# Seven products in the first and the last block of a split FFN: ten more pairs of one kernel

## The chip, the cores and the metric

The kernel runs on one core of one Trainium2 chip. The metric is the device time of one execution in microseconds (us). TensorE is called PE here (its weight loads PEld), VectorE DVE, ScalarE ACT, GpSimd POOL, and the queue that issues the transfers SP.

## The reference

Attention with 8 batches of 576 tokens and 8 heads (half of them with a local mask, half with a strided one) gives a matrix x of 4608 tokens by 512. Behind it stands a feed-forward layer:

```
h = x @ w_in            # 512 -> 2048
g = h * np.cos(h)
return (g @ w_out).astype(np.float32)     # 2048 -> 512
```

All of it is in float32. The change concerns the last line alone.

## The kernel before

The kernel has a long first phase (attention and x @ w_in, which leaves h in DRAM) and a second phase, g @ w_out. The second phase is what the change touches.

**Blocks and pairs.** The 4608 tokens are cut into 18 blocks of 256 (`NTB`), block s being 0 to 17. The 2048 hidden features are cut into 8 pairs of 128-feature tiles (`NF`), pair f being 0 to 7. One step of the second phase, "pair (s, f)", multiplies the 256 tokens by 256 features of g with the 256 by 512 weights of that pair and adds the result to the block's banks in PSUM. The steps stand in the order of `tiles`: all pairs of block 0, then of block 1, and so on.

**Precision.** Every operand is split in a high part (`g_hi`, rounded by ACT) and a low part (`g_lo`, the rest, subtracted by POOL or by DVE), line 188. A product is hi x hi + hi x lo + lo x hi. In `pair` all matmuls with `g_hi` stand first, then `halfway()`, then those with `g_lo`. So `g_lo` is wanted only some way into the pair.

**Eight products or seven.** A pair is a 2 by 2 block product. The plain way takes eight block products; they are issued as 12 matmuls of 512 columns. The other way (Strassen-Winograd) takes seven, issued as 21 matmuls of 256 columns, and needs sums of g and sums of the weights. The weights' sums are made once in the first phase, kept in DRAM (`t_all`) and split by `split_sums`. The sums of g are made for each pair in `gate` by POOL: three additions (lines 681, 682, 685), and then one split of 896 columns in place of one of 512. `seven(s, f)` says which pairs take seven products: those of `SEVEN` (4, 5, 6, 1, 2), not in block 0, not in block 17, and in block 1 only 4, 5 and 6. Pairs 0, 3 and 7 always take eight, and DVE rather than POOL makes their `g_lo` (`BY_VECTOR`).

**What sets the order.** `ahead(at)` starts the stages of `gate` for later pairs while pair `at` is emitted; `LEADS` says how many pairs earlier each stage is started. In the first steps of the second phase, POOL has more to do than gates: `made` places there the splits of the last six weight tiles (`output_weights`, three of them on POOL, at steps 0, 2 and 4) and the splits of the weights' sums for pairs 1 and 2 (`split_sums`, 768 columns and then 256, twice). Program order is the emission order, rearranged by the framework's scheduler before the run; each engine then executes its own list strictly in order. `by_gpsimd` keeps the gates' POOL instructions in the order of the pairs.

**Banks.** A block with any pair of seven has four banks (`lower`, `upper`, `more`, `most`) of the five seats; `shared` adds `more` and `most` up after pair 6, and `store` adds them to `lower` and `upper` on DVE. A block without such a pair has two banks, and `store` copies them out.

Of the kernel before, what the change touches and what calls it, by code (L numbers as in the profile page):

```python
# [19 lines left out]
ALU = mybir.AluOpType  # L20
# [61 lines left out]
NTB = NTOK // TB  # L82
SEVEN = (4, 5, 6, 1, 2)
ROWS = (0, 3, 7)


LEADS = ((6, 4, 3, 2), (7, 4.5, 3.5, 2))
AHEAD = tuple(PER_BATCH - n for n in (20, 17, 13, 10, 7, 3))

BY_VECTOR = (0, 3, 7)  # L90
# [6 lines left out]
SUMMED = (14, 28, 36)  # L97
LATE = 6
# [8 lines left out]
def attention_cos_ffn(ctx, tc, qkl, vl, qkvs, w_in, w_out, eye, eye16, mask_l0, mask_l, mask_s, out):  # L107
    nc = tc.nc
# [484 lines left out]
    def output_weights(room, n, rest=nc.gpsimd):  # L593
        both = room()
        t = weight_tile(n // 2).rearrange("p l m n -> p l (m n)")
        nc.sync.dma_start(out=both, in_=w_all[n])
        yield
        split(both, t[:, 0], t[:, 1], rest=rest)
        wo.append((t[:, 0], t[:, 1]))
        yield  # L600
# [20 lines left out]
    def split_sums(room, n):  # L621

        t = room()
        nc.sync.dma_start(out=t, in_=t_all[n])
        yield
        t = t.rearrange("p (j n) -> p j n", j=4)
        most = wp.tile([P, 2, 3, 2 * P], F32R, name="v")
        split(t[:, :3], most[:, 0], most[:, 1])
        sums[SEVEN[n]] = [(most[:, 0, n], most[:, 1, n]) for n in range(3)]
        yield  # L630
        if n % 3 == 0:
            lasts.append(wp.tile([P, 2, 3, 2 * P], F32R, name="v"))
        last = lasts[-1][:, 0, n % 3], lasts[-1][:, 1, n % 3]
        split(t[:, 3], *last)
        sums[SEVEN[n]].append(last)
        yield
# [1 line left out]
    wo, lasts, gates, sums = [], [], {}, {}  # L638

    def seven(s, f):  # L640
        return 0 < s < NTB - 1 and f in SEVEN[:len(SUMMED) if s == 1 else len(SEVEN)]

    of_gates = []

# [5 lines left out]
    def gate(s, f):  # L650
# [18 lines left out]
        if not seven(s, f):  # L669
            low, pool = (wave, nc.vector) if f in BY_VECTOR else (r, nc.gpsimd)  # L670
            nc.vector.tensor_tensor(out=low, in0=wave, in1=h, op=ALU.mult)
            yield
            g_hi, g_lo = (gp.tile([P, 7 * P], F32R, name=name) for name in ("g_hi", "g_lo"))
            lo = split(low, g_hi[:, :4 * P], g_lo[:, :4 * P], rest=pool)
            if pool is nc.gpsimd:
                by_gpsimd(lo)
            gates[s, f] = g_hi, g_lo
            yield
# [15 lines left out]

    def ahead(at):
        for i, tile in enumerate(tiles):
            if i - at in LEADS[seven(*tile)]:
                next(work[i])

    class Outputs:  # L700
# [17 lines left out]
        def pair(self, f, g_hi, g_lo, halfway):  # L718

            w1, w2 = wo[2 * f:2 * f + 2]  # L720
            if seven(self.s, f):
                left, right = slice(0, 2 * P), slice(2 * P, 4 * P)
                plain = {name: [w[:, part] for w in both] for name, both, part in (
                    ("b11", w1, left), ("b21", w2, left), ("b22", w2, right),
                )}
                products = [
                    (n, plain[w] if w in plain else sums[f][w], (name, at, at + 1)) for n, w, name, at in OUTPUTS
                ]
            else:
                products = [  # L730
                    (2 * n + half, w, (name, 0, 2)) for half, name in enumerate(("lower", "upper"))
                    for n, w in enumerate((w1, w2))
                ]
            groups = [products]
            if self.last and f == NF - 1:
                groups = [products[:2], *(
                    [(n, [w[:, 2 * P * i:2 * P * (i + 1)] for w in both], ("upper", i, i + 1))
                     for n, both, _ in products[2:]] for i in range(2)
                )]
            for group in groups:  # L740
                for n, both, to in group:
                    for w in both:
                        self.add(*to, g_hi[:, n * P:(n + 1) * P], w)
                if group is groups[0]:
                    halfway()
                for n, (w, _), to in group:
                    self.add(*to, g_lo[:, n * P:(n + 1) * P], w)
# [14 lines left out]
        def store(self):  # L762

            rows = out[self.s * TB:(self.s + 1) * TB, :].rearrange("(h p) d -> h p d", h=2)
            for half, name in enumerate(("lower", "upper")):
                o = op.tile([P, 2, 2 * P], F32, name="o", bufs=4)
                if "more" in self.banks:
                    nc.vector.tensor_tensor(
                        out=o, in0=self.banks[name], in1=self.t[:, 2 - 2 * half:4 - 2 * half], op=ALU.add
                    )  # L770
                parts = (slice(0, 1), slice(1, 2)) if self.last and half else (slice(0, 2),)
                for i, part in enumerate(parts):
                    if "more" not in self.banks:
                        copy = nc.scalar.copy if half == i else nc.vector.tensor_copy
                        copy(out=o[:, part], in_=self.banks[name][:, part])
                    nc.sync.dma_start(
                        out=rows[half].rearrange("p (n d) -> p n d", n=2)[:, part], in_=o[:, part]
                    )
# [10 lines left out]
    with ExitStack() as phase:  # L789
# [18 lines left out]
        m, n, o = ((pools[name], name) for name in "mno")  # L808
# [67 lines left out]
        for n in range(2, NF):  # L876
            for i in range(2):
                at = 7 * n + 7 * i // 2 - 13
# [5 lines left out]
        for n in range(NFC - LATE):  # L884
            at = (B - 1) * PER_BATCH + STEP * (n // 2) + 12 + 3 * (n % 2)
# [6 lines left out]
        for b in range(1, B):  # L892
            for i, (summed, made) in enumerate(PREPARED):
                at = (b - 1) * PER_BATCH
# [5 lines left out]
        for slot in range(max(*plan, *steps) + 1):  # L900
            b, at = divmod(slot, PER_BATCH)
            if slot in plan:
                plan[slot]()
            for units_at in bursts.get(slot, ()):
                burst(*units_at)
            for unit in turns.get(slot, ()):
                next(unit)
            for step in steps.get(slot, ()):
                step()
            if b == B - 1:  # L910
                if at == 0:
                    attention.close()
                    sg = ctx.enter_context(tc.tile_pool(
                        name="sg", bufs=3, space=bass.MemoryType.PSUM, side="right", reuse_waits="tile"
                    ))
                    gap(ctx, "to_gates", 56, side="right")
                    gp, hp, rp = (
                        ctx.enter_context(tc.tile_pool(name=name, bufs=bufs, side="right", reuse_waits="tile"))
                        for name, bufs in (("gp", 3), ("hp", 5), ("rp", 3))
                    )  # L920
                if at in AHEAD:
                    ahead(AHEAD.index(at) - len(AHEAD))
# [3 lines left out]
    op = ctx.enter_context(tc.tile_pool(name="op", bufs=2, reuse_waits="tile"))  # L926
# [6 lines left out]
    made = {}  # L933
    for n in range(NFC - LATE, NFC):
        rest = nc.vector if n % 2 else nc.gpsimd
        weights = output_weights(lambda: tp.tile([P, DM], F32, name="both", bufs=LATE), n, rest)
        next(weights)
        made[n + LATE - NFC] = [weights]
    for n in range(len(SUMMED), len(SEVEN)):
        weights = split_sums(lambda: tp.tile([P, 2 * DM], F32, name="t", bufs=2), n)  # L940
        next(weights)
        for i in range(2):
            made.setdefault(LATE + 2 * (n - len(SUMMED)) + i, []).append(weights)
    for i, (s, f) in enumerate(tiles):
        if f == 0:
            block = Outputs(s)
        ahead(i)
        for step in made.get(i, ()):
            next(step, None)
        block.pair(f, *gates.pop((s, f)), partial(ahead, i + 0.5))  # L950
        if "more" in block.banks and f >= max(SEVEN):
            if f == max(SEVEN):
                shared = block.shared()
            next(shared, None)
        if f == NF - 1:
            block.store()
# [94 lines left out]
```

## Time and profile before

| | us |
|---|---|
| timed runs (three) | 852.77, 851.85, 852.76; median 852.76 |
| the profiled execution, its own time | 851.99 |
| its span, first to last instruction | 850.2 |
| outside the span | 1.8 |
| busy: PE / PEld / DVE / ACT / POOL | 839.9 / 783.9 / 554.9 / 529.8 / 536.3 |
| second phase on PE, first to last matmul | 473.42 to 846.64 |

Starts are counted in us from the start of the span. A row of a timeline is one instruction, or several equal ones in a row, with its start and its duration. Instructions on one engine overlap slightly, so what one instruction costs its engine in a full queue is the distance from its start to the start of the next, not its duration.

### The profile page before, as it was taken

Reading aid. Unit: us, or ns where it says so; the run is one execution under the profiler, and the core shown is the slowest. Engines: PE = TensorE matmul, PEld = TensorE weight load, DVE = VectorE, ACT = ScalarE, POOL = GpSimd, SP = SyncE. Lnnn points to the kernel's source line nnn. Section 1 sums busy time; section 2 is a strip of 40 time slices with the busy share of each in tenths; the row PEclk is TensorE's granted clock in tenths of the full one; section 3 lists DMA queues with packets and bytes.
Section 4 is the critical chain, followed back from the end, with each engine's and each line's share of the span. In section 5 each row is a group of like instructions: output and inputs, shape, how many; then the busy total and the mean of one; then the engine's idle time right before and its main releaser. Section 6 shows DMA issues by size and latency. Waiting matters only on the chain.

```text
span 850.2 us, 23162 instructions
## 1 busy us (share of the span) xinstructions
PE 839.9 (99%) x9147; PEld 783.9 (92%) x9147; DVE 554.9 (65%) x1090; ACT 529.8 (62%) x1031; POOL 536.3 (63%) x543
## 2 busy tenths in 40 slices
PE   8899999999999999999999999999999999999998
PEld 5799999999999999999999889999999999999996
DVE  5777655667667576677333667777777776767671
ACT  3766545555445454454457877777777777777772
POOL 3569984415215243163265588999998989898951
PEclk9999999999999999999999999999999999999999
DMA  9788444566674765846465844444444444444330
GB/s 325 230 268 295 148 164 151 190 231 213 209 260 163 246 224 189 301 159 218 176 220 199 281 125 136 124 127 135 125 127 134 125 126 131 130 124 144 116 125 26
DMA packets 91901, 151.82 MB, mean 179 GB/s; under 512 B 8464, under 2 KB 53008, under 8 KB 91792
## 3 DMA queue, kind: packets, MB, share of 16 engines
q1 hardware_dynamic: 91072, 150.11, 53.9%
q8 instruction: 72, 1.18, 0.6%
q10 hardware_dynamic: 720, 0.23, 0.1%
q14 instruction: 37, 0.30, 0.1%
HBM read 96.30 MB, written 54.00 MB: 177 GB/s over the span
## 4 chain that ended last, share of the span: by engine, by line
PE 96%; DMA 1%; POOL 1%; ACT 1%; DVE 1%; issue 1%; SPq 0%
PE q L716 44%; PE m L539 21%; PE n L539 10%; PE m L510 6%; PE o L539 5%; PE acc L342 2%; PE acc L407 2%; PE acc L325 2%; PE acc L394 1%; DMA v<-in_qkvs 1%; PE acc L377 1%; PE m L325 0%; POOL x_lo L188 0%; PE o L394 0%; ACT w L187 0%
## 5 line engine op out<-in xcount | busy, mean ns | idle before, releaser
L716 PE MATMUL q<-w,g_hi 128*128 128x512 f32 (+1 forms) x1000 | 199.9, 338 | 0.0
L716 PEld LDWEIGHTS q<-w,g_hi 128*128 128x128 f32 x1000 | 159.7, 188 | 22.1
L188 POOL TENSOR_TENSOR g_lo<-g,g_hi 128x896 fp32r<-128x896 f32 x78 | 165.1, 2131 | 6.3 <-ACT g_hi L187 6.0
L716 PE MATMUL q<-w,g_lo 128*128 128x512 f32 (+1 forms) x500 | 111.4, 338 | 0.0
L539 PE MATMUL m<-x_hi,v 128*128 128x288 f32 x448 | 109.3, 299 | 0.5 <-ACT m L547 0.5
L539 PE MATMUL m<-x_hi,w 128*128 128x288 f32 x448 | 108.4, 298 | 0.0
L662 DVE SCALAR_TENSOR_TENSOR r<-wave,h_in 128x512 f32<-128x512 int32 x144 | 96.0, 684 | 15.3 <-ACT wave L661 13.9
L664 ACT ACTIVATE wave<-r,quarter 128x512 f32<-128x512 f32 x144 | 98.5, 688 | 6.0 <-DVE r L662 5.9
L187 ACT CAST g_hi<-g 128x896 fp32r<-128x896 f32 x78 | 73.4, 941 | 39.6 <-POOL g L685 27.6
L716 PEld LDWEIGHTS q<-w,g_lo 128*128 128x128 f32 x500 | 82.7, 188 | 10.9
L661 ACT ACTIVATE wave<-h_in 128x512 int32<-128x512 f32 x144 | 83.6, 591 | 7.6 <-DVE g_lo L188 7.4
L716 PE MATMUL q<-v,g_hi 128*128 128x256 f32 x624 | 85.4, 279 | 0.0
L295 POOL TENSOR_TENSOR pn_s<-e_sb,mx 128x324 f32<-128x324 f32 x28 | 21.0, 749 | 100.1 <-DVE mx L293 85.3
L539 PEld LDWEIGHTS m<-x_hi,v 128*128 128x128 f32 x448 | 78.1, 188 | 1.6 <-ACT m L547 0.7
L539 PEld LDWEIGHTS m<-x_hi,w 128*128 128x128 f32 x448 | 78.0, 188 | 0.8
L716 PEld LDWEIGHTS q<-v,g_hi 128*128 128x128 f32 x624 | 78.3, 188 | 0.0
L547 ACT COPY m<-m 128x288 f32<-128x288 f32 x112 | 44.5, 398 | 48.9 <-PE m L539 42.9
L188 DVE TENSOR_TENSOR g_lo<-wave,g_hi 128x512 fp32r<-128x512 f32 x54 | 37.2, 689 | 53.3 <-PE q L716 33.5
L539 PE MATMUL m<-x_lo,v 128*128 128x288 f32 x224 | 66.1, 295 | 0.0
L539 PE MATMUL m<-x_lo,w 128*128 128x288 f32 x224 | 65.9, 294 | 0.0
L682 POOL TENSOR_TENSOR g<-g 128x256 f32<-128x256 f32 x78 | 57.7, 740 | 6.1
L680 DVE TENSOR_TENSOR g<-wave,h_in 128x512 f32<-128x512 f32 x78 | 52.8, 683 | 12.7 <-ACT wave L664 12.7
(138 smaller groups left out, 1996.9 us busy)
## 6 DMA issues: line engine op xcount, KB each, us to landing
h_all<-h SPq DMA_DIRECT2D x128, 288.0 KB, 2.9
h_in<-h_all SPq DMA_DIRECT2D x144, 256.0 KB, 2.8
qk<-in_qkvs SPq DMA_DIRECT2D x28, 324.0 KB, 4.4
out<-o SPq DMA_DIRECT2D x35, 256.0 KB, 3.1
qk<-in_qkl SPq DMA_DIRECT2D x21, 416.0 KB, 4.6
raw<-in_w_in SPq DMA_DIRECT2D x16, 512.0 KB, 4.4
raw<-in_w_out SPq DMA_DIRECT2D x16, 512.0 KB, 5.3
v<-in_vl SPq DMA_DIRECT2D x24, 224.0 KB, 4.3
```

Source lines behind the costliest of these rows:

```text
L187: with_product(cast(out=hi, in_=x))
L188: return rest.tensor_tensor(out=lo, in0=x, in1=hi.bitcast(F32), op=ALU.subtract)
L295: nc.gpsimd.tensor_tensor(out=pn, in0=e, in1=z[:, :n].unsqueeze(2).broadcast_to([P, n, w]), op=ALU.mult)
L510: in_turn(nc.tensor.matmul(self.banks[i, j], a[:, c * P:(c + 1) * P], y[:, c], start=k == 0 and m == 0, stop=k == 1 and m == len(ops) - 1, ...
L539: in_turn(nc.tensor.matmul(bank, a[:, c * P:(c + 1) * P], y[:, c], start=first and i == 0, stop=i == len(ops) - 1, skip_group_check=True,))
L547: nc.scalar.copy(out=t, in_=self.bank[name[0]])
L661: with_product(nc.scalar.activation(out=k, in_=h, func=AF.Copy, scale=1.0 / (2.0 * math.pi), bias=0.25))
L662: nc.vector.scalar_tensor_tensor(out=r, in0=k, scalar=-2.0 * math.pi, in1=h, op0=ALU.mult, op1=ALU.add)
L664: sin = nc.scalar.activation(out=wave, in_=r, func=AF.Sin, bias=quarter)
L680: nc.vector.tensor_tensor(out=g[:, :4].rearrange("p n t -> p (n t)"), in0=wave, in1=h, op=ALU.mult)
L682: by_gpsimd(pool.tensor_tensor(out=g[:, 5:7], in0=g[:, 0:5:4], in1=g[:, 1:2].broadcast_to([P, 2, P]), op=ALU.subtract))
L716: in_turn(nc.tensor.matmul(at, a, w, start=first, stop=True, skip_group_check=True))
```

## The change

Three things are changed. `seven` now takes seven products for pairs 4, 5 and 6 of block 0 as well, and for all five pairs of `SEVEN` in every later block, so for pairs 1 and 2 of block 1 and for all five in the last block: ten pairs more. The stages of the gates of those three pairs of block 0 get a row of leads of their own. The splits of the weights' sums for pairs 1 and 2 stand two steps sooner (steps 4 to 7 rather than 6 to 9), as block 1 now uses them. `store` adds part by part, since the last block stores its upper half in two parts.

```
-LEADS = ((6, 4, 3, 2), (7, 4.5, 3.5, 2))
+LEADS = ((6, 4, 3, 2), (7, 4.5, 3.5, 2), (7, 4, 3.5, 2))
...
     def seven(s, f):
-        return 0 < s < NTB - 1 and f in SEVEN[:len(SUMMED) if s == 1 else len(SEVEN)]
+        return f in SEVEN[:len(SEVEN) if s else len(SUMMED)]
+
+    def leads(s, f):
+        return LEADS[2 if seven(s, f) and not s else seven(s, f)]
...
         for i, tile in enumerate(tiles):
-            if i - at in LEADS[seven(*tile)]:
+            if i - at in leads(*tile):
                 next(work[i])
...
                 o = op.tile([P, 2, 2 * P], F32, name="o", bufs=4)
-                if "more" in self.banks:
-                    nc.vector.tensor_tensor(
-                        out=o, in0=self.banks[name], in1=self.t[:, 2 - 2 * half:4 - 2 * half], op=ALU.add
-                    )
                 parts = (slice(0, 1), slice(1, 2)) if self.last and half else (slice(0, 2),)
                 for i, part in enumerate(parts):
-                    if "more" not in self.banks:
+                    if "more" in self.banks:
+                        nc.vector.tensor_tensor(
+                            out=o[:, part], in0=self.banks[name][:, part],
+                            in1=self.t[:, 2 - 2 * half:4 - 2 * half][:, part], op=ALU.add,
+                        )
+                    else:
...
-            made.setdefault(LATE + 2 * (n - len(SUMMED)) + i, []).append(weights)
+            made.setdefault(LATE - 2 + 2 * (n - len(SUMMED)) + i, []).append(weights)
```

The lists of three engines show where this puts instructions. First POOL before, from the first weight split of the second phase (the one that the trace shows at 477.14 us) on. `w` are weight tiles, `v` the weights' sums, `g_lo` of 512 columns the splits of pairs 4, 5, 6 of block 0 and of pairs 1 and 2 of block 1.

```order
L188 TENSOR_TENSOR w_7936<-both_7935,w_7936 128x512
L188 TENSOR_TENSOR w_7942<-both_7941,w_7942 128x512
L188 TENSOR_TENSOR g_lo_8012<-r_7963,g_hi_8011 128x512
L188 TENSOR_TENSOR w_7948<-both_7947,w_7948 128x512
L188 TENSOR_TENSOR g_lo_8038<-r_7991,g_hi_8037 128x512
L188 TENSOR_TENSOR g_lo_8064<-r_8017,g_hi_8063 128x512
L188 TENSOR_TENSOR v_8129<-t_7953,v_8129 128x768
L188 TENSOR_TENSOR v_8156<-t_7953,v_8156 128x256
L188 TENSOR_TENSOR v_8187<-t_7955,v_8187 128x768
L188 TENSOR_TENSOR g_lo_8145<-r_8095,g_hi_8144 128x512
L188 TENSOR_TENSOR v_8156<-t_7955,v_8156 128x256
L188 TENSOR_TENSOR g_lo_8182<-r_8123,g_hi_8181 128x512
```

Now POOL in the changed kernel, from the same weight split on. `g_7982`, `g_8012` and `g_8044` are the gates of pairs 4, 5 and 6 of block 0 (their three additions are lines 684, 685 and 688 now), `g_lo_8022` is the split of pair 4.

```order
L188 TENSOR_TENSOR w_7938<-both_7937,w_7938 128x512
L684 TENSOR_TENSOR g_7982<-g_7982 128x128
L685 TENSOR_TENSOR g_7982<-g_7982 128x256
L688 TENSOR_TENSOR g_7982<-g_7982 128x128
L684 TENSOR_TENSOR g_8012<-g_8012 128x128
L188 TENSOR_TENSOR w_7944<-both_7943,w_7944 128x512
L685 TENSOR_TENSOR g_8012<-g_8012 128x256
L688 TENSOR_TENSOR g_8012<-g_8012 128x128
L188 TENSOR_TENSOR g_lo_8022<-g_7982,g_hi_8021 128x896
L684 TENSOR_TENSOR g_8044<-g_8044 128x128
L188 TENSOR_TENSOR w_7950<-both_7949,w_7950 128x512
L188 TENSOR_TENSOR v_8089<-t_7955,v_8089 128x768
```

It goes on with the rest of pair 6's additions, the splits of pairs 5 (`g_lo_8054`) and 6 (`g_lo_8078`), and the additions of pair 1 of block 1 (`g_8149`) around the second set of weights' sums.

```order
L685 TENSOR_TENSOR g_8044<-g_8044 128x256
L188 TENSOR_TENSOR v_8131<-t_7955,v_8131 128x256
L688 TENSOR_TENSOR g_8044<-g_8044 128x128
L188 TENSOR_TENSOR g_lo_8054<-g_8012,g_hi_8053 128x896
L188 TENSOR_TENSOR g_lo_8078<-g_8044,g_hi_8077 128x896
L684 TENSOR_TENSOR g_8149<-g_8149 128x128
L188 TENSOR_TENSOR v_8171<-t_7957,v_8171 128x768
L685 TENSOR_TENSOR g_8149<-g_8149 128x256
L188 TENSOR_TENSOR v_8131<-t_7957,v_8131 128x256
L688 TENSOR_TENSOR g_8149<-g_8149 128x128
```

So the first set of weights' sums now stands ahead of the split of pair 5 of block 0, where it stood behind the split of pair 6. Behind these rows come the additions of pair 2 of block 1, the splits of its pairs 1 and 2, the additions of pairs 4 and 5, the split of pair 4, the additions of pair 6, and the splits of pairs 5 and 6.

At the end of DVE's list there stood one copy of the last part, behind the last gate's work:

```order
L671 TENSOR_TENSOR r_12562<-wave_12563,h_in_12516 128x512
L662 SCALAR_TENSOR_TENSOR r_12584<-wave_12585,h_in_12542 128x512
L671 TENSOR_TENSOR wave_12585<-wave_12585,h_in_12542 128x512
L188 TENSOR_TENSOR g_lo_12619<-wave_12585,g_hi_12618 128x512
L775 COPY o_12667<-q3_12523 128x256
```

and now stand the sums of the last block and three additions (the last row is two instructions):

```order
L757 TENSOR_TENSOR t_12785<-q0_12628,t_12785 128x256
L759 TENSOR_TENSOR t_12785<-q4_12639,t_12785 128x512
L762 TENSOR_TENSOR t_12785<-q4_12639,t_12785 128x256
L773 TENSOR_TENSOR o_12808<-q1_12598,t_12785 128x512
L773 TENSOR_TENSOR o_12811<-q3_12603,t_12785 128x256 x2
```

ACT's two copies at the end (one of 512 columns, one of 256) are gone.

## Rows read from the trace of the kernel before

**Rows 1.** The page: span, busy time of the engines, granted PE clock by slices.

```profile
span 850.2 us, 23162 instructions
PE 839.9 (99%) x9147; PEld 783.9 (92%) x9147; DVE 554.9 (65%) x1090; ACT 529.8 (62%) x1031; POOL 536.3 (63%) x543
PEclk9999999999999999999999999999999999999999
```

**Rows 2.** The page: the chain that ended last, share of the span by engine.

```profile
PE 96%; DMA 1%; POOL 1%; ACT 1%; DVE 1%; issue 1%; SPq 0%
```

**Rows 3.** Waits of PE, whole span, longest and shortest: total, times, longest.

```profile
PE acc L342 <- issue: 2.0, 1, 2.0
...
PE m L325 <- issue: 0.2, 1, 0.2
```

**Rows 4.** Timeline of PE: starts of pairs (0, 4) and (0, 7).

```profile
484.52 2.03 PE L716 MATMUL q<-w,g_hi 128*128 128x512 f32 x8
...
492.93 2.01 PE L716 MATMUL q<-w,g_hi 128*128 128x512 f32 x8
```

**Rows 5.** Timeline of PE: block 1, pairs 1, 3, 4, 5 and 7.

```profile
498.40 2.03 PE L716 MATMUL q<-w,g_hi 128*128 128x512 f32 x8
...
504.01 2.01 PE L716 MATMUL q<-w,g_hi 128*128 128x512 f32 x8
...
506.76 0.86 PE L716 MATMUL q<-w,g_hi 128*128 128x256 f32 x6
...
508.40 0.51 PE L716 MATMUL q<-w,g_lo 128*128 128x256 f32 x3
...
509.22 0.86 PE L716 MATMUL q<-w,g_hi 128*128 128x256 f32 x6
...
514.12 2.01 PE L716 MATMUL q<-w,g_hi 128*128 128x512 f32 x8
```

**Rows 6.** Timeline of POOL, start of the second phase.

```profile
477.14 1.29 POOL L188 TENSOR_TENSOR w<-both,w 128x512 fp32r<-128x512 f32 x1 [3.70 <-ACT w L187]
...
481.78 1.44 POOL L188 TENSOR_TENSOR g_lo<-r,g_hi 128x512 fp32r<-128x512 f32 x1 [0.26 <-ACT g_hi L187]
...
494.21 1.85 POOL L188 TENSOR_TENSOR v<-t,v 128x768 fp32r<-128x768 f32 x1 [2.75 <-ACT v L187]
496.02 1.30 POOL L188 TENSOR_TENSOR g_lo<-r,g_hi 128x512 fp32r<-128x512 f32 x1
497.28 0.73 POOL L188 TENSOR_TENSOR v<-t,v 128x256 fp32r<-128x256 f32 x1
497.97 1.29 POOL L188 TENSOR_TENSOR g_lo<-r,g_hi 128x512 fp32r<-128x512 f32 x1
499.22 0.46 POOL L681 TENSOR_TENSOR g<-g 128x128 f32<-128x128 f32 x1
499.76 0.74 POOL L682 TENSOR_TENSOR g<-g 128x256 f32<-128x256 f32 x1
...
500.99 0.46 POOL L681 TENSOR_TENSOR g<-g 128x128 f32<-128x128 f32 x1
...
502.77 2.13 POOL L188 TENSOR_TENSOR g_lo<-g,g_hi 128x896 fp32r<-128x896 f32 x1
504.86 0.47 POOL L681 TENSOR_TENSOR g<-g 128x128 f32<-128x128 f32 x1
```

**Rows 7.** Timeline of DVE: its second weight split of the second phase.

```profile
481.22 0.85 DVE L188 TENSOR_TENSOR w<-both,w 128x512 fp32r<-128x512 f32 x1 [1.04 <-ACT w L187]
```

**Rows 8.** Windows, a block with five pairs of seven: length, busy PE, PEld, DVE, ACT, POOL.

```profile
552.00:572.49 20.49, 20.49 (x143) 19.02 (x143) 14.67 (x25) 15.87 (x25) 18.60 (x21) 1.00 0.44 129
```

**Rows 9.** Timelines of PE, DVE and ACT at the end.

```profile
846.24 0.40 PE L716 MATMUL q<-w,g_lo 128*128 128x256 f32 x2
...
846.68 0.42 DVE L775 COPY o<-q 128x256 f32<-128x256 f32 x1 [7.65 <-PE q L716]
...
847.14 0.37 ACT L775 COPY o<-q 128x256 f32<-128x256 f32 x1 [1.29 <-DVE o L775]
```

## The prediction

> **What bounds the kernel now.** I read the page first. PE is busy for 839.9 of 850.2 us, the chain that ended last is PE for 96%, and the granted clock stands at its full level in every slice [rows 1, 2]. The waits of PE say where it stood still: the longest wait is 2.0 us, the shortest listed 0.2, and none belongs to the lines of the second phase [rows 3]. So the second phase is a row of matmuls without a gap, and what a pair costs is the distance between the starts of neighbouring pairs. Three pairs of eight products (4, 5, 6 of block 0) take 492.93 - 484.52 = 8.41 us, 2.80 each [rows 4]; pairs 1 and 2 of block 1 take 504.01 - 498.40 = 5.61, 2.80 each again [rows 5]. Three pairs of seven take 514.12 - 506.76 = 7.36, 2.45 each [rows 5]. That PE never waits doesn't say how near the others are to making it wait. The windows do: in a block with five pairs of seven, POOL is busy 18.6 of 20.5 us, ACT 15.9, DVE 14.7 [rows 8]. POOL has 1.9 us in hand in a settled block. In the first block it has work beside the gates, and the timeline of POOL is what the rest hangs on.
>
> **What PE gains.** Ten pairs go from 2.80 to 2.45 us: three in block 0 (8.41 - 7.36 = 1.05), two in block 1 (5.61 - 2 x 2.45 = 0.70), five in the last block (5 x 0.35 = 1.75). Sum: 3.5 us. It lies wholly on the path, if nothing has to be waited for.
>
> **What POOL must do for it, instruction by instruction.** From the split at 477.14 us on [rows 6], I lay POOL's new list end to end. That start is set by ACT's half of the split (the row's releaser) and doesn't move. Prices are distances between starts in stretches where POOL had no pause [rows 6]: a split of 512 columns 499.22 - 497.97 = 1.25; of 256 497.97 - 497.28 = 0.69; of 768 496.02 - 494.21 = 1.81; of 896 504.86 - 502.77 = 2.09; a gate's three additions 500.99 - 499.22 = 1.77. In these 1.77 each later addition waits 0.08 for the one before (499.22 + 0.46 to 499.76), which falls away where another instruction stands between them.
>
> When does PE want the result? A pair of seven reaches its matmuls with `g_lo` 508.40 - 506.76 = 1.64 after its start [rows 5].
>
> - Pair (0, 4): POOL has done one weight split, its additions, pair 5's additions with a second weight split among them, and the gate's split: 1.25 + 1.77 + 1.69 + 1.25 + 2.09 = 8.05, so 485.19. PE wants it at 484.52 + 1.64 = 486.16. In time.
> - Pair (0, 5): ahead of its split now stand pair 6's additions (1.61, cut in three pieces), the third weight split 1.25, and the first set of weights' sums, 1.81 + 0.69. With its own 2.09: 485.19 + 1.61 + 1.25 + 2.50 + 2.09 = 492.64. PE wants it at 484.52 + 2.45 + 1.64 = 488.61. **PE stands still for 4.0 us.**
> - Pairs (0, 6), (1, 1), (1, 2), (1, 4): POOL ends at 494.7, 502.7, 504.8 and 510.4. PE, 4.0 late, wants them at 495.1, 503.0, 505.4 and 510.7. In time by 0.3 to 0.7.
> - Pair (1, 5): behind (1, 4) stand pair 6's additions and its own split, 1.77 + 2.09, so 514.28. Without any stall PE would want it at 506.76 - 1.05 - 0.70 + 2.45 + 1.64 = 509.10.
>
> The whole list from 477.14 to there is 37.14 us: three weight splits 3.75, eight sets of additions 8 x 1.77 - 5 x 0.08 = 13.76, the weights' sums 5.00, seven splits 14.63. POOL never pauses in it, so stalls aren't added but set by its end: 514.28, plus 0.04 for the last split's tail (2.13 long, 2.09 apart), against 509.10 makes 5.22 us in all. The handover to PE I take at 0.04, as from PE to DVE at the end [rows 9]; the trace doesn't show what PE needs to restart, and I bound it by one run of two matmuls, 0.40 [rows 9]. Behind (1, 5) PE is 5.3 late, POOL's 18.6 per block fits in PE's 20.5 [rows 8], and nothing waits any more.
>
> Behind the waiting matmul all of PE is queued, and with it the banks and the `g_hi` buffers, for which ACT waits. POOL's next splits need buffers of pairs that PE has left already, so POOL isn't held up by the stall.
>
> **A price between two bounds.** In the same stretch one split of POOL took 1.44 instead of 1.29 [rows 6], beside a weight split of DVE [rows 7]. Three such DVE splits fall in POOL's list: 0 to 0.45 us, and I take the one that the row shows, 0.15. The Trainium skill (GPSIMD Engine Reference, Specifications) says that POOL shares its SBUF interfaces with VectorE and contends with VectorE instructions that have two SBUF inputs. By that all three would be slowed, and the sum would be 0.3 higher; one row of this case agrees, with its 0.15 us.
>
> **Edits at nothing.** DVE's additional sums in block 0 and the last block replace copies; DVE and ACT have 4.6 us and more to spare per block of this form [rows 8]. If that cover were gone, a late sum would hold back a bank and add at most its own 0.4 to 0.7. Transfers keep their order in SP's list, so none moves past another. At the end, DVE's copy of 0.42 and ACT's of 0.37 follow each other [rows 9]; now two additions on DVE do, each bounded by that 0.42 as the same size: 0, within 0.1. The addition for the lower half lies beside the last matmuls; uncovered it would cost about twice that 0.42.
>
> **Sum.** -3.50 + 5.22 + 0.04 + 0.15 = +1.9 us. On the profiled execution, 851.99 (its span 850.2 and 1.8 around it), that is 853.9. The median of the runs lies 0.77 above that execution; on its scale the forecast is 852.76 + 1.9 = 854.7.
>
> **The rivals.**
>
> *PE loses its clock in the stall.* No row shows PE still for over 2.0 us, and through that its granted clock stayed at 2.4 GHz [rows 1, 3]; now it is still for 4.0. If the clock fell to 1.2 GHz, each 2.45 us pair would take 4.9 while that lasts. I bound it by two pairs: up to 4.9 lost, of which the 1.2 that PE would wait at (1, 5) anyway is free, so 0 to 3.7 more: 854.7 to 858.4. For it: the stall is twice the longest wait. Against it: the clock never moved here. Chance 0.23. The Trainium skill (TensorE: Matmul & The Clock Gate, the HAM clock gate) says that an idle PE is set back to half its clock and must be busy for a while to regain it; by that rule the time would come out above my forecast. No run shown here tests it at this length.
>
> *Faster: POOL's list is shorter than its rows laid end to end.* If neighbouring splits and additions overlapped more in the new order, the stall would shrink. It decides at one point: PE gains 3.5, so the list must shrink from 37.1 us to 33.5 for the stall to fall to 1.7 and the kernel to come out faster by 0.2%; with no stall at all it is 852.76 - 3.5 = 849.3. For it: POOL's spans are rough, and two instructions of one kind already overlap by 0.04. Against it: the prices are distances between starts, the pure overlap is in them, and the same stretch of the old kernel holds the densest POOL work and gave them. Time 849.3 to 851.0. Chance 0.13.
>
> *The two cancel.* The list is shorter by 1 to 3.5 us, for instance because the interleaving frees more than the 0.08 per cut. Time 851.0 to 853.6. Chance 0.06.
>
> That the change doesn't do what it says is excluded by the lists: ten more sets of additions stand in POOL's.
>
> **How the numbers follow.** The forecast has 0.58. Its own range comes from the bounds: POOL's handovers all free and no contention (8 x 0.16 - 0.40 = 0.88 and 0.15 less, so +0.9), or all three contentions and the slowest restart (0.30 and 0.36 more, so +2.6): 853.6 to 855.4. A measurement of this kernel tells about 0.2%, or 1.7 us, from no change. Most of the forecast's range lies above 852.76 + 1.7 = 854.5, but not much: I give 0.36 to slower and 0.22 to the same. With the clock rival: slower 0.36 + 0.23 = 0.59; same 0.22 + 0.06 = 0.28; faster 0.13. The range reaches down into the faster rival's upper end and up into the clock rival's: 851.2 to 857.2.
>
> **What would show it.** Right: a wait of PE for POOL's `g_lo` of about 4 us in pair 5 of block 0 (near 488.6) and one of about 1.2 in pair 5 of block 1, POOL without a pause from 477 to 514, pairs of 2.45 us in block 0 and the last block, the second phase 1.9 us longer. Wrong: no wait of PE in the second phase (then POOL's prices were too high), a granted clock below full behind the stall, POOL pausing inside its list (then something else, an ACT cast or a DVE product, is late), or a longer tail after the last matmul than 3.6 us.

## The result, and the profile after

The changed kernel is slower: 857.39 us (median of five runs, 855.68 to 858.56) against 852.66 (851.85 to 852.77) for the kernel before, a ratio of 1.0055 (95% interval 1.0043 to 1.0066), 4.7 us. A second timing (e8 below) gave 856.95 against 852.26, 1.0060 (1.0048 to 1.0072). Four runs in a slower state of the chip (one of e3, one of e10, two of the kernel before beside e1, e3, e7 and e8) are left out of all medians and ratios. The direction was forecast; the size wasn't: 854.7 was the forecast, 857.2 the upper end of its range.

The page of the changed kernel, parts 1, 2 and 4: POOL has entered the chain that ended last with 3%, PE has lost 4 points of it, and one slice of the clock is no longer full (against [rows 1, 2]).

```profile
span 855.6 us, 23394 instructions
PE 839.9 (98%) x9237; PEld 788.9 (92%) x9237; DVE 559.5 (65%) x1099; ACT 532.4 (62%) x1030; POOL 561.4 (66%) x573
PEclk9999999999999999999999989999999999999999
...
PE 92%; POOL 3%; DMA 1%; DVE 1%; ACT 1%; issue 1%; SPq 0%; DVEq 0%; POOLq 0%; ACTq 0%
```

The waits of PE, longest first (total, times, longest). There is a new row on top, of the second phase, where [rows 3] had none:

```profile
PE q L719 <- POOL g_lo L188: 5.0, 1, 5.0
PE acc L342 <- issue: 1.7, 1, 1.7
```

The timeline of PE shows where it stands. Pair (0, 4) starts at 485.09, (0, 5) at 487.79, (0, 6) at 496.24 and (0, 7) at 500.60. Pair (0, 4) already takes 2.70 us instead of 2.45:

```profile
485.09 0.86 PE L719 MATMUL q<-w,g_hi 128*128 128x256 f32 x6
...
487.79 0.87 PE L719 MATMUL q<-w,g_hi 128*128 128x256 f32 x6
488.50 1.10 PE L719 MATMUL q<-v,g_hi 128*128 128x256 f32 x8
494.57 1.01 PE L719 MATMUL q<-w,g_lo 128*128 128x256 f32 x3 [4.97 <-POOL g_lo L188]
495.38 1.05 PE L719 MATMUL q<-v,g_lo 128*128 128x256 f32 x4
496.24 1.48 PE L719 MATMUL q<-w,g_hi 128*128 128x256 f32 x6
497.51 1.91 PE L719 MATMUL q<-v,g_hi 128*128 128x256 f32 x8
499.22 0.84 PE L719 MATMUL q<-w,g_lo 128*128 128x256 f32 x3
499.86 0.90 PE L719 MATMUL q<-v,g_lo 128*128 128x256 f32 x4
500.60 2.02 PE L719 MATMUL q<-w,g_hi 128*128 128x512 f32 x8
```

Three things are to be seen. The wait is in the pair and at the matmuls that were forecast, but 5.0 us long instead of 4.0. The second wait of the forecast, 1.2 us at pair (1, 5), is missing: PE reaches its `g_lo` matmuls after POOL has made them. And what follows the first wait runs slowly: the seven `g_lo` matmuls of (0, 5) take 496.24 - 494.57 = 1.67 us instead of 0.82, and pair (0, 6) 500.60 - 496.24 = 4.36 instead of 2.45. The windows name the cause (columns as in [rows 8]; behind the engines the granted clock):

```profile
490.00:492.00 2.00, 0.00 (x0) 0.00 (x0) 0.91 (x2) 0.60 (x1) 2.00 (x3) 1.00 0.58 161
492.00:494.00 2.00, 0.00 (x0) 0.00 (x0) 0.03 (x1) 1.42 (x2) 2.00 (x3) 0.90 0.29 101
494.00:495.00 1.00, 0.43 (x2) 0.43 (x3) 0.66 (x1) 0.45 (x1) 1.00 (x2) 0.50 0.00 0
...
499.00:500.00 1.00, 1.00 (x6) 1.00 (x6) 0.73 (x2) 0.16 (x1) 1.00 (x2) 0.50 0.81 220
500.00:501.00 1.00, 1.00 (x7) 0.96 (x6) 0.07 (x1) 0.47 (x2) 1.00 (x3) 0.78 0.25 51
501.00:505.00 4.00, 4.00 (x19) 3.26 (x19) 3.77 (x7) 3.93 (x6) 3.25 (x3) 1.00 0.43 124
```

PE stands still from 489.6 on; while it does, the clock goes from 2.4 to 1.2 GHz. The shares 0.90 and 0.78 put the fall at 493.6 and the return at 500.4, so 6.8 us at half.

The timeline of POOL has no pause from 477.76 to 502.4, so none up to the split that PE waits for. The forecast had none up to 514; there is one of 0.59 us, the last row below. Three of POOL's instructions are longer than those of their size in [rows 6]:

```profile
479.57 1.23 POOL L685 TENSOR_TENSOR g<-g 128x256 f32<-128x256 f32 x1
...
481.72 1.76 POOL L188 TENSOR_TENSOR w<-both,w 128x512 fp32r<-128x512 f32 x1
...
487.18 1.30 POOL L188 TENSOR_TENSOR w<-both,w 128x512 fp32r<-128x512 f32 x1
488.43 2.28 POOL L188 TENSOR_TENSOR v<-t,v 128x768 fp32r<-128x768 f32 x1
...
492.44 4.14 POOL L188 TENSOR_TENSOR g_lo<-g,g_hi 128x896 fp32r<-128x896 f32 x2
...
502.95 4.23 POOL L188 TENSOR_TENSOR g_lo<-g,g_hi 128x896 fp32r<-128x896 f32 x2 [0.59 <-ACT g_hi L187]
```

They are 0.49, 0.47 and 0.43 over 0.74, 1.29 and 1.85. DVE's timeline has its three weight splits there:

```profile
479.52 0.68 DVE L188 TENSOR_TENSOR w<-both,w 128x512 fp32r<-128x512 f32 x1
...
481.49 0.82 DVE L188 TENSOR_TENSOR w<-both,w 128x512 fp32r<-128x512 f32 x1
...
487.44 1.59 DVE L188 TENSOR_TENSOR w<-both,w 128x512 fp32r<-128x512 f32 x1
```

Each of the three long instructions of POOL started while a DVE split ran. The split of POOL that was already at work when the third DVE split came (487.18) kept its 1.30, and there the DVE split took 1.59 instead of 0.68.

The pause at 502.4 has its cause in ACT's list. ACT's casts of `g_hi` stand behind a copy of the banks of block 0, and that copy waited for the slow matmuls:

```profile
500.53 0.37 ACT L756 COPY t<-q 128x256 f32<-128x256 f32 x1 [1.37 <-PE q L719]
```

The end, against [rows 9]. PE's timeline has the last matmuls:

```profile
851.46 0.40 PE L719 MATMUL q<-w,g_lo 128*128 128x256 f32 x2
```

In DVE's, the two additions follow them directly:

```profile
851.89 0.75 DVE L773 TENSOR_TENSOR o<-q,t 128x256 f32<-128x256 f32 x2 [0.19 <-PE q L719]
```

From the last matmul to the end of the span it is 855.57 - 851.86 = 3.71 us now, 850.20 - 846.64 = 3.56 before.

### The profile page after: what moved, and what is told of

It reads as the page before. It is cut to its first block, busy times and chain, and to the rows that moved or that the text cites. A ratio compares the mean times of both kernels' runs of the same rounds, so it can differ in the third digit from the quotient of the medians.

```text
span 855.6 us, 23394 instructions
## 1 busy us (share of the span) xinstructions
PE 839.9 (98%) x9237; PEld 788.9 (92%) x9237; DVE 559.5 (65%) x1099; ACT 532.4 (62%) x1030; POOL 561.4 (66%) x573
## 4 chain that ended last, share of the span: by engine, by line
PE 92%; POOL 3%; DMA 1%; DVE 1%; ACT 1%; issue 1%; SPq 0%; DVEq 0%; POOLq 0%; ACTq 0%
PE q L719 42%; PE m L539 21%; PE n L539 10%; PE m L510 6%; PE o L539 5%; PE acc L342 2%; PE acc L325 2%; PE acc L407 2%; PE acc L394 1%; DMA v<-in_qkvs 1%; PE acc L377 1%; POOL w L188 1%; POOL g_lo L188 0%; POOL x_lo L188 0%; DMA both<-w_all 0%
## 5 line engine op out<-in xcount | busy, mean ns | idle before, releaser
L188 POOL TENSOR_TENSOR g_lo<-g,g_hi 128x896 fp32r<-128x896 f32 x88 | 186.1, 2130 | 8.3 <-ACT g_hi L187 7.9
L719 PE MATMUL q<-w,g_hi 128*128 128x256 f32 (+1 forms) x980 | 188.8, 331 | 0.0
L719 PEld LDWEIGHTS q<-w,g_hi 128*128 128x128 f32 x980 | 153.0, 189 | 18.3
L719 PE MATMUL q<-w,g_lo 128*128 128x256 f32 (+1 forms) x490 | 106.5, 331 | 5.0 <-POOL g_lo L188 5.0
L187 ACT CAST g_hi<-g 128x896 fp32r<-128x896 f32 x88 | 82.7, 941 | 45.6 <-POOL g L688 34.7
L719 PE MATMUL q<-v,g_hi 128*128 128x256 f32 x704 | 97.2, 280 | 0.0
L719 PEld LDWEIGHTS q<-w,g_lo 128*128 128x128 f32 x490 | 80.0, 190 | 14.4 <-POOL g_lo L188 5.3
L719 PEld LDWEIGHTS q<-v,g_hi 128*128 128x128 f32 x704 | 89.2, 190 | 0.0
L188 DVE TENSOR_TENSOR g_lo<-wave,g_hi 128x512 fp32r<-128x512 f32 x54 | 37.2, 690 | 61.4 <-PE q L719 41.9
L685 POOL TENSOR_TENSOR g<-g 128x256 f32<-128x256 f32 x88 | 65.6, 745 | 6.7
L683 DVE TENSOR_TENSOR g<-wave,h_in 128x512 f32<-128x512 f32 x88 | 59.3, 682 | 13.7 <-ACT wave L667 12.7
```

The lines of the kernel that those rows point to most:

```text
L187: with_product(cast(out=hi, in_=x))
L188: return rest.tensor_tensor(out=lo, in0=x, in1=hi.bitcast(F32), op=ALU.subtract)
L683: nc.vector.tensor_tensor(out=g[:, :4].rearrange("p n t -> p (n t)"), in0=wave, in1=h, op=ALU.mult)
L685: by_gpsimd(pool.tensor_tensor(out=g[:, 5:7], in0=g[:, 0:5:4], in1=g[:, 1:2].broadcast_to([P, 2, P]), op=ALU.subtract))
L719: in_turn(nc.tensor.matmul(at, a, w, start=first, stop=True, skip_group_check=True))
```

## The experiments

Two measures stand in the table. The ratio comes from whole runs, each beside runs of the kernel before on its chip. The second phase is read from each profile, from the start of its first matmul to the end of its last (373.22 us before); it leaves out the first phase, which no kernel changes and which varies by more than what is to be told apart (the second phase starts between 472.61 and 474.43 us).

| kernel | median, before on its chip | ratio (95%) | second phase, against before |
|---|---|---|---|
| the change | 857.39, 852.66 | 1.0055 (1.0043-1.0066) | 377.87, +4.65 |
| e8: the change again | 856.95, 852.26 | 1.0060 (1.0048-1.0072) | 376.65, +3.43 |
| e4: stall filled | 855.50, 851.88 | 1.0049 (1.0037-1.0061) | 376.32, +3.10 |
| e5: DVE reads nothing | 855.35, 851.88 | 1.0037 (1.0025-1.0049) | 375.42, +2.20 |
| e6: both | 854.71, 851.88 | 1.0036 (1.0024-1.0048) | 374.99, +1.77 |
| e7: old steps | 855.78, 852.26 | 1.0043 (1.0031-1.0056) | 376.76, +3.54 |
| e3: block 0 alone | 856.22, 852.26 | 1.0049 (1.0035-1.0062) | 375.35, +2.13 |
| e1: last block alone | 851.46, 852.26 | 0.9989 (0.9980-0.9997) | 371.49, -1.73 |
| e2: last block and block 1 | 849.91, 851.88 | 0.9978 (0.9969-0.9987) | 370.74, -2.48 |
| e10: e2 again | 850.26, 852.14 | 0.9974 (0.9964-0.9985) | 370.76, -2.46 |
| e9: e2 and one pair of block 0 | 851.07, 852.14 | 0.9990 (0.9981-0.9999) | 371.90, -1.32 |

The theory after the result: the stall of the forecast is real, DVE's weight splits make POOL's list 1.4 us longer where I had priced 0.15, and the clock falls in the stall. The main rivals: the clock's fall costs nothing, since POOL's list sets the time anyway; the three long instructions come from the transfers of that stretch; and the sooner steps of the weights' sums, not the amount of work, are what makes POOL late.

**e4, the stall filled.**

```
                 if group is groups[0]:
                     halfway()
+                    if (self.s, f) == (0, 5):
+                        bank = pools["q"].tile([P, 512], F32, name="q4")
+                        for _ in range(20):
+                            in_turn(nc.tensor.matmul(
+                                bank, warm, warm.unsqueeze(1).broadcast_to([P, 4, P]), start=True, stop=True
+                            ))
```

> The changed kernel with 20 matmuls of zeros, 512 columns each, issued into the free bank between the g_hi and the g_lo matmuls of pair (0, 5), so that PE works through most of the stall (20 x 0.216 = 4.3 us, estimated from 0.23 us between starts of 512-column matmuls). They are extra work. POOL's list is the same, word for word. Theory: the clock fell because PE was idle for 5 us. Then no slice is below full clock, the rest of pair (0, 5) and pair (0, 6) take 0.8 and 2.45 us again instead of 1.67 and 4.36, which gives back 2.8 us; of that POOL's list, which goes on as before, takes back 1.0 to 1.6 at pair (1, 5): 1.2 to 1.8 us less than the changed kernel, a ratio of 1.0034 to 1.0042 to the kernel before. Rival: the clock costs nothing, because POOL's list alone sets when block 1 goes on; then PE waits 2.8 us longer at (1, 5) or sooner and the ratio stays at 1.0055. Second rival: something else lowers the clock there; then it falls again.

The timeline of PE, with the filling matmuls and the two waits:

```profile
488.87 4.49 PE L752 MATMUL q<-warm 128*128 128x512 bf16 x20
494.03 0.62 PE L719 MATMUL q<-w,g_lo 128*128 128x256 f32 x3 [0.67 <-POOL g_lo L188]
...
515.61 0.62 PE L719 MATMUL q<-w,g_lo 128*128 128x256 f32 x3 [0.81 <-POOL g_lo L188]
```

The window over the rest of the pair and what follows it:

```profile
494.00:500.00 6.00, 5.97 (x40) 5.49 (x41) 4.64 (x9) 4.25 (x8) 6.00 (x6) 1.00 0.21 51
```

The clock holds, and a second wait of 0.81 us comes up at pair (1, 5), where the forecast had one of 1.2. PE's useful work resumes no sooner (`g_lo` at 494.03), and still the second phase is 1.55 us shorter than the change's. So the fall costs 1.55 us of the 2.76 that the slow matmuls took; the other 1.2 would have been waited at (1, 5). Against e8, whose clock was low half as long (below), it is 0.33. The rival "costs nothing" falls for the first profile. The ratio, 1.0049, is above the 1.0034 to 1.0042 expected, and its interval overlaps the change's, so the times of whole runs don't settle it. Their clocks point the same way: the mean granted clock of a whole run is 0.996 to 1.000 in the six of e4 and 0.991 to 0.996 in the eleven of the change (e8's among them).

**e5, DVE reads nothing in its weight splits.** The low part of three weight tiles is left out.

```
+        if rest is nc.vector:
+            with_product(nc.scalar.copy(out=t[:, 0], in_=both))
+            nc.vector.memset(t[:, 1].bitcast(F32), 0.0)
+        else:
-        split(both, t[:, 0], t[:, 1], rest=rest)
+            split(both, t[:, 0], t[:, 1], rest=rest)
```

> The changed kernel in which the low part of DVE's three weight splits of the second phase (tiles 11, 13 and 15) isn't subtracted but written as zeros, so that DVE reads nothing there; the low part of these three tiles is left out of the result. POOL's list is the same. Theory: DVE's weight splits lengthened three of POOL's instructions (1.23, 1.76 and 2.28 us instead of 0.74, 1.30 and 1.85). Then these three are back at their prices, PE's wait in pair (0, 5) falls from 5.0 to 3.6 us, and the ratio from 1.0055 by 1.0 to 1.6 us, to 1.0036 to 1.0043, if the clock falls as before; lower if it doesn't. Rival: the transfers that land in that stretch (1.05 of the DMA engines' time from 480 to 485 us) lengthened them; then they stay long, the wait stays at 5.0 us and the ratio at 1.0055.

The same three instructions in POOL's timeline:

```profile
479.84 0.74 POOL L689 TENSOR_TENSOR g<-g 128x256 f32<-128x256 f32 x1
...
481.50 1.30 POOL L188 TENSOR_TENSOR w<-both,w 128x512 fp32r<-128x512 f32 x1
...
487.75 1.87 POOL L188 TENSOR_TENSOR v<-t,v 128x768 fp32r<-128x768 f32 x1
```

And PE's wait:

```profile
493.49 0.97 PE L723 MATMUL q<-w,g_lo 128*128 128x256 f32 x3 [3.84 <-POOL g_lo L188]
```

All three are back at their prices, and the transfers were not touched. That settles the contention: DVE's weight splits are its cause. The wait falls to 3.84, against 3.6 expected of this run and 4.0 in the forecast. The clock (0.89 of full from 492 to 494 us, 0.50 from 494 to 496) goes to half at its end, 0.1 us after PE has resumed, and stays there for 3.4 us.

**e6, both edits.** The low part of the same three weight tiles is left out.

> Both edits at once: matmuls of zeros in the stall and no subtraction in DVE's three weight splits (the low part of three weight tiles is left out). Theory: what is left is the forecast's own sum without contention and without the clock, 3.50 gained and 5.26 lost, so +1.8 us, a ratio of 1.0018 to 1.0024, with the end of POOL's list at pair (1, 5) setting it. Rivals: if either effect was not the cause, that part stays, 1.0035 or more.

The second phase is 1.77 us longer than before. That is the forecast's own sum without its contention term, -3.50 + 5.26 = +1.76. By the ratio of whole runs, 1.0036, it would be the rival's case (1.0035 or more); the forecast's sum is borne out by the trace of the second phase alone. In PE's timeline one wait for POOL is left, at pair (1, 5); in (0, 5) the filled 4.5 us cover the stall.

```profile
515.09 0.62 PE L723 MATMUL q<-w,g_lo 128*128 128x256 f32 x3 [0.68 <-POOL g_lo L188]
```

The whole runs came out 2.8 us above before. The profiled one lies 3.5 above the profiled execution of the kernel before. Besides the 1.77, the tail after the last matmul (4.0 us against 3.56) accounts for 0.4, a second phase that starts 0.8 later (474.24 against 473.42) for 0.8, and time outside the span (2.3 against 1.8) for 0.5.

**e7, the old steps for the weights' sums.**

```
-            made.setdefault(LATE - 2 + 2 * (n - len(SUMMED)) + i, []).append(weights)
+            made.setdefault(LATE + 0 + 2 * (n - len(SUMMED)) + i, []).append(weights)
```

> The whole change but for the steps: the splits of the weights' sums stay at steps 6 to 9 instead of 4 to 7. Theory: PE's loss is set by how much POOL has to do up to the split of pair (1, 5), which is the same work in another order; so PE waits less in (0, 5) (2.5 to 3.0 us) and again in block 1, 5.2 to 6.6 in all, and if the clock holds the second phase is as long as with the filled stall, 3.1 us over before (ratio 1.0036), with no useless matmul. Rival: the sums' splits ahead of pair (0, 5) are what makes the change slow; then it is within 0.6 us of the kernel before or faster.

PE's timeline, its two longest waits:

```profile
492.20 0.62 PE L719 MATMUL q<-w,g_lo 128*128 128x256 f32 x3 [2.66 <-POOL g_lo L188]
...
516.12 0.61 PE L719 MATMUL q<-w,g_lo 128*128 128x256 f32 x3 [1.12 <-POOL g_lo L188]
```

The windows at and behind the first wait:

```profile
492.00:494.00 2.00, 1.80 (x12) 1.80 (x13) 1.49 (x3) 1.89 (x4) 2.00 (x2) 0.81 0.26 92
494.00:496.00 2.00, 2.00 (x11) 2.00 (x10) 1.91 (x4) 2.00 (x5) 2.00 (x3) 0.50 0.10 17
```

The wait in (0, 5) is nearly halved and the second phase is about as long as that of the change, +3.54 against +3.43 and +4.65; a part of what PE doesn't wait in block 0 it waits in block 1. All its waits for POOL, four of them, are 4.4 us together, less than the 5.2 to 6.6 expected. The rival of the sooner steps falls. That the order of POOL's list moves the stall and its length sets the end is seen in the traces: from POOL's first weight split to PE's restart at (1, 5) it is 516.12 - 477.72 = 38.40 us here and 515.61 - 477.21 = 38.40 in e4, in two orders. The clock didn't hold, though. The 0.81 puts its fall at 493.2, 1.0 us after PE had resumed, so the +3.1 without a fall wasn't seen here.

**e8, the change again.**

> The changed kernel once more, on the chip of this call. Every theory: the wait of 5 us in pair (0, 5), the clock at half behind it, the second phase 4.65 us over before, ratio 1.0043 to 1.0066.

The wait is the same, 5.0 us at the same matmuls. The low clock is shorter, about 3.4 us by two windows:

```profile
494.00:496.00 2.00, 1.42 (x6) 1.42 (x7) 0.68 (x1) 1.44 (x3) 2.00 (x2) 0.56 0.00 0
496.00:498.00 2.00, 2.00 (x13) 2.00 (x12) 1.45 (x3) 1.88 (x4) 2.00 (x3) 0.59 0.00 0
```

The second phase is 1.2 us shorter than in the first profile. So how long the clock stays low differs from one execution of the change to the next, and the time with it.

**e3 and e1, block 0 and the last block each alone.** The first new line is e3's, the second e1's, the third stands in both.

```
-        return f in SEVEN[:len(SEVEN) if s else len(SUMMED)]
+        return f in ((4, 5, 6) if s == 0 else (4, 5, 6) if s == 1 else SEVEN if s < NTB - 1 or False else ())
...
+        return f in (() if s == 0 else (4, 5, 6) if s == 1 else SEVEN if s < NTB - 1 or True else ())
...
+            made.setdefault(LATE + 0 + 2 * (n - len(SUMMED)) + i, []).append(weights)
```

> Block 0's part alone: pairs 4, 5 and 6 of block 0 take seven products; block 1 and the last block as before, the weights' sums split at their old steps, so behind pair 6's split. Theory: POOL reaches the split of pair (0, 5) 2.5 us sooner than in the change, so PE waits 2.5 to 3.0 us there, with DVE's weight splits still lengthening POOL's instructions; with 1.05 gained the second phase is 1.5 to 2.0 us longer than before if the clock holds through that idle time, and 3 to 4.7 longer if it falls: ratio 1.0018 to 1.0024, or 1.0035 to 1.0055. Rival: without the sums ahead of it the split of (0, 5) is in time, and 1.05 us are gained: ratio 0.9988.

> The last block's part alone: five pairs of seven products there, everything else as before. Theory: nothing waits, 5 x 0.35 = 1.75 us off the second phase (373.22 us from the first to the last of its matmuls), less 0.2 to 0.4 at the end, where the runs so far showed that much more after the last matmul: ratio 0.9979 to 0.9984. Rival: the additions at the end cost as much as the pairs gain; then 1.0.

The wait in e3's timeline of PE:

```profile
492.59 0.62 PE L719 MATMUL q<-w,g_lo 128*128 128x256 f32 x3 [2.65 <-POOL g_lo L188]
```

Block 0 alone waits 2.65 us, with the clock at full before and behind it, and its second phase is 2.13 us longer: three pairs that gain 1.05 cost three times that. That is a little over the 1.5 to 2.0 expected with the clock held. Its runs lie 4.0 us above before, more than the profile shows. The profiled run (855.36) is the shortest; its mean granted clock is 0.998, that of the three others 0.994 to 0.996, so the clock was low for longer in them. Where was not traced. The last block alone gains 1.73 us in the second phase, five times 0.35, with no wait. In whole runs 0.80 of it is left; the tail (3.7 us) takes 0.2, and the rest is within the interval. The ratio, 0.9989, misses the 0.9979 to 0.9984 expected.

**e2, e9 and e10: where POOL's room ends.** The first new line is that of e2 and e10, the second e9's.

```
-        return f in SEVEN[:len(SEVEN) if s else len(SUMMED)]
+        return f in (() if s == 0 else (4, 5, 6, 1, 2) if s == 1 else SEVEN if s < NTB - 1 or True else ())
...
+        return f in ((4,) if s == 0 else (4, 5, 6, 1, 2) if s == 1 else SEVEN if s < NTB - 1 or True else ())
```

> The change without block 0: five pairs of the last block and pairs 1 and 2 of block 1 take seven products, the splits of the weights' sums stand two steps sooner as in the change. Theory: POOL's list has three additions' sets and three long splits less ahead of block 1 (3 x (1.77 + 2.09 - 1.25) = 7.8 us), so it catches up and PE never waits: 7 x 0.35 = 2.45 us gained, less up to 0.2 at the end, ratio 0.9971 to 0.9974. Rival: the sooner splits and the two pairs of block 1 alone make PE wait there by 1 us or more; then 0.998 to 1.0.

> The version without block 0 (seven pairs of the ten), plus pair 4 of block 0 alone: an eighth pair. Theory: POOL's work up to the split of pair (1, 5) decides, not where it stands. From 477.14 us on the list is the change's 37.1 us less two pairs of block 0 (2 x (1.77 + 2.09 - 1.25) = 5.2), plus what DVE's weight splits add (1.4): 33.3, so its end is at 510.5 to 511.2, and PE wants it 0.35 sooner than without the eighth pair, at 509.8: a wait of 0.7 to 1.4 us at (1, 5), none in block 0. The eighth pair gains 0.35 and loses 0.7 to 1.4: second phase 1.4 to 2.1 us under before, against 2.48 with seven pairs. Rival: POOL has room for one more pair; then 2.8 us under before and no wait.

> The version without block 0 once more, beside the one with the eighth pair on the same chip. Theory: second phase 2.48 us under before, no wait of PE in it, ratio 0.9969 to 0.9987.

Seven pairs, without block 0, gain 2.48 and 2.46 us in the second phase, 7 x 0.35, and PE waits nowhere in it. That is the fastest version, 0.9978 and 0.9974 of the kernel before. An eighth pair, in block 0, gives about half of it back: the wait comes up at (1, 5), nine pairs later, as it does when POOL's list is laid out for it. PE's timeline of e9:

```profile
508.34 0.87 PE L719 MATMUL q<-w,g_hi 128*128 128x256 f32 x6
...
511.24 0.62 PE L719 MATMUL q<-w,g_lo 128*128 128x256 f32 x3 [1.09 <-POOL g_lo L188]
...
512.16 0.86 PE L719 MATMUL q<-w,g_hi 128*128 128x256 f32 x6
```

The pair takes 512.16 - 508.34 = 3.82 us instead of 2.45, 1.37 more for a wait shown as 1.09: the idle time alone is short of what a wait costs, since the first matmuls behind it are slower (0.62 against 0.51 in a pair without a wait) and the ends of those ahead of it are modelled. -2.48 - 0.35 + 1.37 = -1.46; with pair (1, 1), which is 0.12 late, -1.34; measured -1.32, just short of the 1.4 to 2.1 expected.

## Why the prediction had the sign and missed the size

- **What PE gains, right.** 0.35 us a pair: -1.73 for five (e1), -2.48 for seven (e2).
- **POOL's list sets the stall, right, in place and in mechanism.** The wait stands in pair (0, 5) at the `g_lo` matmuls, and POOL works without a pause up to it. The list's length and not its order decides (e4, e7). From its first split to PE's restart at (1, 5) the forecast had 37.14 + 0.04 + 0.04 = 37.2 us; e6, without contention and with the clock held, has 515.09 - 478.02 = 37.1. That the second phase came out at +1.77 against +1.76 is closer than such a list can promise; the last hundredths are luck.
- **The price between two bounds, wrong; this is the term that was mis-sized.** I took 0.15 us for DVE's weight splits, with 0.45 for all three as the upper bound. They cost 0.49 + 0.47 + 0.43 = 1.4, and e4 less e6 is 1.33 on the second phase. Two of the three stand ahead of pair (0, 4) and use up the 0.97 by which it was forecast to be in time; it loses 0.25. The row that I priced by, 1.44 instead of 1.29, showed a split that DVE met only in part. DVE's first split of the old kernel met no POOL instruction at all, since POOL stood idle from 478.43 to 480.22, and its third met one but was itself the one that took longer. In the new list POOL has the next instruction ready at once, and it starts while the DVE split runs. An overlap that a half-idle engine shows is not the price in a full queue. The Trainium skill (GPSIMD Engine Reference, Specifications) names the ground, SBUF interfaces shared with VectorE instructions that have two SBUF inputs; the trace agrees, with three times 0.45 us. DVE's other instructions here, which read a PSUM tile and one SBUF tile, lengthened none. DVE's first and third split in the kernel before, and the POOL splits next to them:

```profile
478.89 0.68 DVE L188 TENSOR_TENSOR w<-both,w 128x512 fp32r<-128x512 f32 x1
...
485.31 0.96 DVE L188 TENSOR_TENSOR w<-both,w 128x512 fp32r<-128x512 f32 x1
```

```profile
480.22 1.30 POOL L188 TENSOR_TENSOR w<-both,w 128x512 fp32r<-128x512 f32 x1 [1.78 <-DVE r L662]
...
484.43 1.30 POOL L188 TENSOR_TENSOR g_lo<-r,g_hi 128x512 fp32r<-128x512 f32 x1
```

- **The clock, at nothing in the sum and taken as the less likely rival; it fell.** I gave it 0.23 since the clock never moved in the old trace, but no wait there was longer than 2.0 us. It cost 1.55 us in the first profile and 0.33 in the second, within the 0 to 3.7 of the rival, and the 1.2 us that the rival called free were free (e4). In the first profile it is the larger half of the miss. The Trainium skill (TensorE: Matmul & The Clock Gate, the HAM clock gate) says that an idle PE is set back to half its clock. In the 5.0 us of both profiles the traces agree. They also show the fall behind the 3.84 of e5 and the 2.66 of e7, and none around the 2.65 of e3, so the length of the wait alone doesn't tell.
- **"The clock never moved here" held for one execution.** Of the twelve profiles, eight (all but those of the kernel before, the change, e9 and e10) have the clock at half once in the first phase, from 22 to 25 us on, around a wait of PE of 1.6 to 2.3 us that the other four have too (1.7 to 2.0); e1 and e2, whose second phases wait nowhere, are among them. The kernel before isn't exempt: in eight of its sixteen runs beside e4 the mean granted clock is 0.996 to 0.998, in the others 1.000. The traced execution happened to be one without a fall.
- **POOL held up by the stall: not by the wait, but by the slow matmuls behind it.** I had said that it isn't. In the first profile POOL pauses for 0.59 us at 502.4, in e8 nowhere. It cost PE nothing, since PE was later still.
- **The edits priced at nothing, nearly.** The end costs 0.15 us in the change (3.71 against 3.56), 0.1 having been allowed; 0.15 to 0.25 in the other versions with additions at the end and about 0.45 in e5 and e6.

Three of the four signs of being wrong that the prediction names were seen: a clock below full behind the stall, a pause in POOL's list, and a tail longer than 3.6 us.

In one sum, for the first profile's second phase: -3.50 gained, +5.26 of stall as forecast, +1.33 of contention, +1.55 of clock make +4.64; measured +4.65. The last two terms are differences between measured versions, so the agreement tests the first two; the contention has its own witness in POOL's rows (1.4), the clock in e8, where its term is 0.33. The forecast's own 1.9 had the first two and a tenth of the third.

Open: in all versions but e7, whole runs compare worse with before than their second phases do, by 0.1 us in the change and by 0.25 (e9) to 1.8 (e3) in the others. A part may be the clock's fall in the first phase (in e6 from about 24.5 to 28 us), which comes with some executions and not others; a part lies outside the span (up to 3.6 us in a run of e4, 1.7 to 1.9 in those of the kernel before). Whether that is all of it wasn't measured.

## What to carry to other kernels

When PE has no gap, write out the queue of the engine that feeds it, instruction by instruction with distances between starts, and compare its end with the moment PE wants it: this gave the place of the stall here, and its size in the one profile without contention and a fall of the clock. Price a contended instruction by what it costs in a full queue, and look in the new order which neighbours will meet. Ask of more than one execution whether the clock holds. And a wait of some microseconds on PE should be priced with the clock's fall behind it, not beside it as an unlikely case. The better version spends the feeding engine's room and stops one pair before it is gone.

## What the runs showed of the hardware

- A DVE subtraction with two SBUF operands lengthened the POOL instruction that started while it ran by 0.43 to 0.49 us in the change, whatever its kind (an addition of 256 columns, splits of 512 and 768). A POOL split that was already at work when it came kept its 1.30, and the DVE subtraction itself took longer: 1.59 us in the change and 0.96 in the kernel before, instead of 0.68.
- The granted clock went to half about 4 us after PE's last matmul (489.6 to 493.6) and came back 5.9 us after it resumed (494.57 to 500.4); in e8 it fell later and came back after some 3.4 us. Twenty matmuls of zeros in the gap kept it at full.
- Waits of 2.65 and 2.66 us in the same place, in e3 and e7, left the clock alone once and were followed by half the clock once, from 1.0 us after PE had resumed; a wait of 0.40 stood one pair ahead in e7. In the first phase the clock went to half around a wait of 1.6 to 2.3 us in eight of twelve profiles; the other four have the wait (1.7 to 2.0 us) and no fall.
